# Gated MLP behind block attention on one core: a contiguous place for the low words' bits, and other places in the hand-written order for loads, scores and one weight part

## The chip, the cores and the metric

The kernel runs on one core of a Trainium2 chip. The metric is the device time of one execution in microseconds (us); the version before takes 528.58 us, the median of three runs (528.41 to 528.75). TensorE, VectorE, ScalarE, GpSimd and SyncE are called PE, DVE, ACT, POOL and SP, as in the profile; PEld is PE's loading of weights. SP issues all DMAs.

## What is computed

```python
# 8 batches, 8 heads, 576 tokens, head size 64: attention inside chunks of 64 tokens
scores = scale * np.matmul(q_c, k_c.transpose(0, 1, 2, 4, 3))
attn = np.exp(scores - np.max(scores, axis=-1, keepdims=True))
x = np.matmul(attn / (np.sum(attn, axis=-1, keepdims=True) + 1e-09), v_c)   # -> (8, 576, 512)
# then, for every batch
h = gelu_tanh(x @ w_in)                       # w_in (512, 1024), given in 64-bit floats
u, v = (h[..., :512], h[..., 512:])
v_n = (v - mean(v)) / np.sqrt(var(v) + 1e-06) * g_ln
v_s = np.einsum('ts,bsd->btd', w_sg, v_n) + b_sg[None, :, None]
out = x + (u * v_s) @ w_out                   # w_out (512, 512), given in 64-bit floats
```

## The kernel before

**Tiles and units.** Attention works on 36 tiles of 128 tokens, numbered 0 to 35; a batch has four and a half. The MLP works batch by batch, in units of 12 or 14 weight passes on PE: `v_unit` (L440, matmul L451), `u_unit` (L479, L488), `s_unit` (L500, L508) and `o_unit` (L520, L531). Each product of two 32-bit numbers is made of three passes with high and low parts, hence the names ending in `h` and `l`. A unit's result lies in one of three buffers named `pm` in PSUM, and the unit three places later waits until ACT or DVE has emptied it.

**The start.** Batches 0 and 1 are worked off by a list, START (L45). A letter and a number are a step: `v13` is `v_unit` of batch 1, part 3, and likewise `u`, `s`, `o`. `S` scores a tile (L313 or L321, then softmax), `T` transposes it, `O` multiplies by V (L409) and keeps the result (`keep`, L418: `xh`, `xl` and `xf`, on ACT and DVE). `P5` is `S` for tiles 5 and 6 together, `Q5` is `O` for both. `L`, `W`, `w` load, begin and end one of four parts of `w_in`'s v half, `X` and `x` begin and end one of its u half. `Y0` to `Y7` load and convert the eight parts of `w_out` (`o_w`, L213). `A8` loads tiles up to 8 where that has not been done. `D` is a run of spare matmuls (L577). From batch 2 on, loops run the units and a table, SLOTS, hangs attention steps behind them; neither is touched.

**Loads.** `att_load` (L281) takes one of four buffers `qkv_t`. `scores` (L550) loads two tiles ahead of the tiles that it scores, once the first batch is past. The parts of `w_out` go through the same four buffers (`st`, L219). A buffer is taken when its last reader is done, and SP issues in order: what waits for a buffer holds up every later DMA.

**Weights in 64-bit floats.** `pair_begin` (L152) makes of one part's words a 32-bit number `f`, its power of two `p`, and in L165 16-bit words `q` with the bits that `f` has lost. `pair_end` (L167) sums them on PE in four passes (L177): `f`, `q`, `p`, and minus the high part; ACT then writes `win_l` (L178). A u unit needs its own part's `win_l`.

**What orders the engines.** START gives the order in which steps are recorded. When the program is built, a scheduler places the instructions of each engine by readiness, so an engine's row differs from the list in places; on the chip, each engine then works its row off strictly in order.

Of the kernel before, what the change touches and what calls it, by code (L numbers as in the profile page):

```python
# [14 lines left out]
U16 = mybir.dt.uint16  # L15
BF16 = mybir.dt.bfloat16
AF = mybir.ActivationFunctionType
ALU = mybir.AluOpType
# [3 lines left out]
B, H, S, D = 8, 8, 576, 64  # L22
P = 128
# [20 lines left out]

START = """  # L45
L0 A0 A1 L1 S0 L2 T0 D11 A2 W0 A3 W1 L3 A4 S1 W2 S2 w0 w1 W3 T1 O0 w2 S3 O1 T2 w3 D14 O2 T3 S4 M0 v00 X0 O3 G0 T4 v01
A8 O4 x0 X1 v02 x1 X2 v03 v04 u00 g0 g1 x2 g2 u01 g3 X3 u02 x3 g4 u03 P5 s00 s01 T5 P7 s02 T6 Q5 s03 T7 T8 v10 Q7 v11
Y0 Y1 v12 Y2 v13 Y3 u10 Y4 u11 Y5 u12 Y6 u13 Y7 A10 s10 s11 P9 s12 s13 o00 T9 o01 T10 o02 o03 Q9 P11 o10 o11 T11 o12
T12 Q11 S13 o13 T13
"""  # L50

PE_TILES = 5
# [28 lines left out]
def block_attention_gated_mlp(ctx: ExitStack, tc: tile.TileContext, qkv, w_in, w_out, w_sg, g_ln, b_sg, out):  # L81
    nc = tc.nc
# [43 lines left out]
    def high_word(f, hw):  # L126

        nc.scalar.activation(f.bitcast(F32), hw.bitcast(F32), AF.Abs, scale=2.0**16)  # L130
        nc.vector.tensor_scalar(f.bitcast(F32), f.bitcast(F32), ZERO64, TOP64, op0=ALU.max, op1=ALU.min)
        nc.vector.tensor_scalar(f, f, 4, 1, op0=ALU.logical_shift_left, op1=ALU.logical_shift_right)
        nc.vector.scalar_tensor_tensor(f, hw, -0x80000000, f, op0=ALU.bitwise_and, op1=ALU.bitwise_or)
# [20 lines left out]
    def pair_begin(n, st):  # L154

        pair = st[:, : 2 * n].rearrange("p (n w) -> p n w", w=2)
        f, p = st[:, 2 * n : 3 * n], st[:, 3 * n : 4 * n]  # L160
        high_word(f, pair[:, :, 1])
        nc.vector.tensor_scalar(p, f, -0x800000, None, op0=ALU.bitwise_and)

        q, top = st[:, : 2 * n].bitcast(U16)[:, 1::4], p.bitcast(U16)[:, 1::2]
        nc.vector.scalar_tensor_tensor(q, q, 9, top, op0=ALU.logical_shift_right, op1=ALU.bitwise_or)  # L165

    def pair_end(n, hi, lo, st):  # L167

        f = st[:, 2 * n : 3 * n].bitcast(F32)
        p, q = st[:, 3 * n : 4 * n].bitcast(BF16)[:, 1::2], st[:, : 2 * n].bitcast(BF16)[:, 1::4]  # L170
        ps = ps_m.tile([P, 2, 512], F32, name="pm")[:, 0, :n]
        shape = lambda a: a.rearrange("p (k c) -> p k c", k=hi.shape[1]) if len(hi.shape) == 3 else a
        nc.scalar.mul(hi, shape(f), -1.0)
        terms = [(ident, f), (low[0], q), (low[1], p), (ident_r, hi)]
        for i, (a, c) in enumerate(terms):
            out_ps = shape(ps) if c is hi else ps
            nc.tensor.matmul(out_ps, a, c, start=(i == 0), stop=(i == len(terms) - 1))  # L177
        nc.scalar.mul(lo, shape(ps), -1.0)  # L178
# [14 lines left out]
    def v_w_end(kt):  # L193
        pair_end(DH, win_h[:, kt, DH:], win_l[:, kt, DH:], staged["v", kt])
        u_w_load(kt)
# [61 lines left out]
    def load_misc():  # L257
        nc.sync.dma_start(out=g_bc, in_=g_ln.broadcast_to([P, DH]))
# [4 lines left out]
    last = [((b + 1) * S - 1) // P for b in range(B)]  # L263
# [6 lines left out]
    def next_bank():  # L270
        turn[0] ^= 1
        return banks[:, turn[0]].rearrange("p (hp s) -> p hp s", hp=HP)
# [30 lines left out]
    def att_scores(*tiles):  # L303

        scs = []
        for i, t in enumerate(tiles):
            qt = state[t]
            if t < PE_TILES:
                sc = ps_m.tile([P, 2, H, D], F32, name="pm")[:, 0]
                for h in range(H):  # L310
                    for c in range(2):
                        r = slice(c * D, (c + 1) * D)
                        nc.tensor.matmul(sc[r, h, :], qt[r, 0, h, :], qt[r, 1, h, :], start=True, stop=True)  # L313
            else:


                sc = banks[:, :, i * HP * D : (i + 1) * HP * D].rearrange("p c (hp s) -> p c hp s", hp=HP)
                for h in range(H):
                    for c in range(2):
                        r, o = slice(c * D, (c + 1) * D), slice((h + c) % 2 * D, ((h + c) % 2 + 1) * D)  # L320
                        nc.tensor.matmul(sc[o, c, h // 2, :], qt[r, 0, h, :], qt[r, 1, h, :], start=True, stop=True)  # L321
            scs.append(sc)
        for t, sc in zip(tiles, scs):
            softmax_begin(t, sc)
        for t in tiles:
            softmax_end(t)

    def softmax_begin(t, sc):
        qt = state[t]
        nmax = small.tile([P, H], F32, name="nmax")  # L330
        by_slot = lambda a: a if t < PE_TILES else a.rearrange("p (c hp) s -> p c hp s", c=2)
        nc.vector.tensor_reduce(  # L332
            nmax if t < PE_TILES else nmax.rearrange("p (c hp) -> p c hp", c=2), sc, axis=AX.X, op=ALU.max, negate=True
        )
        pt = att.tile([P, H, D], F32, name="pt", bufs=3)
        den = small.tile([P, H], F32, name="den")
        scale = 1.0 / math.sqrt(D)
        if t in ACT_SOFTMAX:
            nc.vector.tensor_scalar(nmax, nmax, scale, None, op0=ALU.mult)
            for h in range(H):  # L340
                col = slice(h, h + 1)
                src = sc[:, h, :] if t < PE_TILES else sc[:, h // HP, h % HP, :]
                nc.scalar.activation(pt[:, h, :], src, AF.Exp, bias=nmax[:, col], scale=scale, accum_out=den[:, col])  # L343
        else:
            nc.vector.tensor_tensor(
                by_slot(pt), sc, by_slot(nmax.unsqueeze(2).broadcast_to([P, H, D])), op=ALU.add
            )
            nc.scalar.activation(pt, pt, AF.Exp, scale=scale)
        state[t] = (qt, pt, den)

    def softmax_end(t):
        qt, pt, den = state[t]
        if t not in ACT_SOFTMAX:
            nc.vector.tensor_reduce(den, pt, axis=AX.X, op=ALU.add)
        nc.vector.tensor_scalar(den, den, SM_EPS, None, op0=ALU.add)
        nc.vector.reciprocal(den, den)  # L356
        (nc.gpsimd if t > last[1] else pick(f"n{t}")).tensor_tensor(pt, pt, den.unsqueeze(2).broadcast_to([P, H, D]), op=ALU.mult)  # L357
        state[t] = (qt, pt)
# [25 lines left out]
    def att_out(*tiles):  # L384

        xos = []
        pm = ps_m.tile([P, 2, 512], F32, name="pm") if tiles[0] >= PE_TILES else None
        for i, t in enumerate(tiles):
            qt, ptT = state.pop(t)
            if t < PE_TILES:  # L390
                vt = qt[:, 2, :, :].rearrange("p (c hp) d -> p c hp d", c=2)
                xo = next_bank()
                for hp in range(HP):
                    for c in range(2):
                        for j in range(2):
                            r = slice(j * D, (j + 1) * D)
                            nc.tensor.matmul(
                                xo[r, hp, c * D : (c + 1) * D], vt[r, c, hp, :], ptT[r, hp, c * D : (c + 1) * D],
                                start=True, stop=True,
                            )  # L400
                xo = xo.rearrange("p hp (c s) -> p c hp s", c=2)
            else:

                xo = pm[:, :, i * HP * D : (i + 1) * HP * D].rearrange("p c (hp s) -> p c hp s", hp=HP)
                for h in range(H):
                    for c in range(2):
                        j, place = (h + c) % 2, c * HP + h // 2
                        r, o = slice(j * D, (j + 1) * D), slice(h % 2 * D, (h % 2 + 1) * D)
                        nc.tensor.matmul(  # L409
                            xo[o, c, h // 2, :], qt[r, 2, place, :], ptT[r, place].rearrange("p a s -> p (a s)"),  # L410
                            start=True, stop=True,
                        )
            xos.append(xo)
        for t, xo in zip(tiles, xos):
            keep(t, xo)
# [129 lines left out]
    def ahead(t):  # L545
        while loaded[0] <= min(t, NT - 1):
            att_load(loaded[0])
            loaded[0] += 1

    def scores(*tiles):  # L550
        if tiles[0] > last[0]:
            ahead(tiles[-1] + 2)
        att_scores(*tiles)

    def att_slots(b, n):
# [9 lines left out]

    steps = {
        "L": v_w_load, "M": lambda k: load_misc(), "W": v_w_begin, "w": v_w_end, "X": u_w_begin, "x": u_w_end, "A": ahead,
        "S": scores, "T": att_transpose, "O": att_out, "P": lambda t: scores(t, t + 1), "Q": lambda t: att_out(t, t + 1),
    }
    for name, f in zip("vuso", (v_unit, u_unit, s_unit, o_unit)):  # L570
        steps[name] = (lambda f: lambda k: f(k // 10, k % 10))(f)
# [65 lines left out]
```

## Time and profile before

The profiled execution took 529.45 us; its span, from the first to the last instruction, is 527.7 us, and every time of the trace counts from the span's start.

| | value |
|---|---|
| median of three runs | 528.58 us |
| profiled execution | 529.45 us |
| its span | 527.7 us |
| mean granted PE clock | 0.990 |
| ACT busy, share of the span | 275.3 us, 52% |
| POOL busy, share of the span | 71.9 us, 14% |
| DMA | 46.58 MB, mean 88 GB/s |

An engine's busy time is the sum of its instructions' spans. In a timeline each row gives a start, a length, the engine, the line and the operation; a bracket at its end gives how long the engine had been idle and what released it. Matmuls are pipelined: a unit's cost on PE is the distance between its first start and the next unit's first start.

### The profile page before, as it was taken

Reading aid. Unit: us, or ns where it says so; the run is one execution under the profiler, and the core shown is the slowest. Engines: PE = TensorE matmul, PEld = TensorE weight load, DVE = VectorE, ACT = ScalarE, POOL = GpSimd, SP = SyncE. Lnnn points to the kernel's source line nnn. Section 1 sums busy time; section 2 is a strip of 40 time slices with the busy share of each in tenths; the row PEclk is TensorE's granted clock in tenths of the full one; section 3 lists DMA queues with packets and bytes.
Section 4 is the critical chain, followed back from the end, with each engine's and each line's share of the span. In section 5 each row is a group of like instructions: output and inputs, shape, how many; then the busy total and the mean of one; then the engine's idle time right before and its main releaser. Section 6 shows DMA issues by size and latency. Waiting matters only on the chain.

```text
span 527.7 us, 12465 instructions
## 1 busy us (share of the span) xinstructions
PE 507.2 (96%) x5278; PEld 467.3 (89%) x5278; DVE 341.6 (65%) x704; ACT 275.3 (52%) x509; POOL 71.9 (14%) x75
## 2 busy tenths in 40 slices
PE   5989989799999989999999999999999999999997
PEld 5576869689999879998999889998999899998996
DVE  5978808877977676758655495768556495636042
ACT  4677634665434687535564367445654468324110
POOL 0032300011011131103110040103010040102000
PEclk9999989899999999999999999999999999999999
DMA  8676000412346700333214402251305300020002
GB/s 331 241 228 193 0 1 1 121 42 82 85 121 210 207 21 14 108 106 105 71 52 130 134 9 55 67 151 62 106 16 155 117 0 2 2 91 1 1 1 89
DMA packets 49595, 46.58 MB, mean 88 GB/s; under 512 B 35202, under 2 KB 39554, under 8 KB 49540
## 3 DMA queue, kind: packets, MB, share of 16 engines
q1 hardware_dynamic: 49540, 45.80, 28.8%
q8 instruction: 41, 0.67, 0.5%
q14 instruction: 14, 0.11, 0.1%
HBM read 36.34 MB, written 9.44 MB: 87 GB/s over the span
## 4 chain that ended last, share of the span: by engine, by line
PE 77%; DVE 10%; ACT 6%; issue 2%; POOL 2%; DMA 1%; DVEq 0%; SPq 0%; ACTq 0%; POOLq 0%
PE pm L508 21%; PE pm L488 19%; PE pm L531 17%; PE pm L451 14%; PE pm L409 3%; PE banks L321 2%; POOL sm L460 1%; ACT pt L343 1%; DMA qkv_t<-qkv 1%; DVE blocks L371 1%; DVE wsg L165 1%; DVE wout L165 1%; DVE nmax L332 1%; DVE sm L457 1%; ACT xh L94 1%
## 5 line engine op out<-in xcount | busy, mean ns | idle before, releaser
L508 PE MATMUL pm<-wsg,v 128*128 128x288 f32 x768 | 108.2, 296 | 0.0
L508 PEld LDWEIGHTS pm<-wsg,v 128*128 128x128 f32 x768 | 103.8, 189 | 0.5
L531 PE MATMUL pm<-gh,wout 128*128 128x288 f32 x512 | 92.1, 297 | 0.0
L531 PEld LDWEIGHTS pm<-gh,wout 128*128 128x128 f32 x512 | 76.0, 189 | 0.5
L357 POOL TENSOR_TENSOR pt<-pt,den 128x512 f32<-128x512 f32 x28 | 29.8, 1076 | 235.7 <-DVE den L356 125.8
L488 PE MATMUL pm<-xh,win_l 128*128 128x288 f32 x256 | 56.1, 301 | 3.8 <-ACT win_l L178 2.3
L460 POOL TENSOR_TENSOR sm<-sm,neg_half 128x1 f32<-128x1 f32 x36 | 35.3, 980 | 166.2 <-DVE sm L459 165.6
L531 PE MATMUL pm<-gl,wout 128*128 128x288 f32 x256 | 55.7, 296 | 0.0
L488 PE MATMUL pm<-xh,win_h 128*128 128x288 f32 x256 | 55.7, 299 | 0.0
L488 PE MATMUL pm<-xl,win_h 128*128 128x288 f32 x256 | 55.5, 298 | 0.0
L451 PE MATMUL pm<-win_h,xl 128*128 128x512 f32 x128 | 52.4, 409 | 2.1 <-DVE xl L97 2.1
L94 ACT CAST gh<-gt 128x576 fp32r<-128x576 f32 x32 | 21.5, 673 | 61.0 <-DVE gt L512 60.8
L451 PE MATMUL pm<-win_l,xh 128*128 128x512 f32 x128 | 51.5, 403 | 0.0
L451 PE MATMUL pm<-win_h,xh 128*128 128x512 f32 x128 | 51.5, 402 | 0.0
L512 DVE TENSOR_TENSOR gt<-pm,u 128x576 f32<-128x576 f32 x32 | 24.2, 756 | 37.9 <-PE pm L508 37.9
L488 PEld LDWEIGHTS pm<-xh,win_l 128*128 128x128 f32 x256 | 41.9, 191 | 5.2 <-ACT win_l L178 2.7
L539 DVE TENSOR_TENSOR ot<-pm,xf 128x576 f32<-128x576 f32 (+1 forms) x33 | 24.1, 734 | 28.9 <-PE pm L531 28.8
L488 PEld LDWEIGHTS pm<-xh,win_h 128*128 128x128 f32 x256 | 41.6, 191 | 0.0
L531 PEld LDWEIGHTS pm<-gl,wout 128*128 128x128 f32 x256 | 41.5, 189 | 0.1
L488 PEld LDWEIGHTS pm<-xl,win_h 128*128 128x128 f32 x256 | 41.6, 191 | 0.0
L457 DVE BATCH_NORM_STATS2 sm<-hs 128x6 f32<-128x512 f32 x36 | 24.7, 687 | 25.1 <-ACT hs L454 25.0
L97 DVE TENSOR_TENSOR xl<-pm,xh 128x512 fp32r<-128x512 f32 (+1 forms) x34 | 21.8, 641 | 26.3 <-ACT xh L94 26.3
(121 smaller groups left out, 843.1 us busy)
## 6 DMA issues: line engine op xcount, KB each, us to landing
qkv_t<-qkv SPq DMA_DIRECT2D x32, 512.0 KB, 4.5
out_dram<-ot SPq DMA_DIRECT2D x31, 288.0 KB, 2.2
qkv_t<-qkv SPq DMA_DIRECT2D x124, 64.0 KB, 3.7
qkv_t<-qkv SPq DMA_DIRECT2D x3, 768.0 KB, 9.7
wsg<-w_in SPq DMA_DIRECT2D x4, 512.0 KB, 4.1
wout<-w_in SPq DMA_DIRECT2D x4, 512.0 KB, 6.1
st<-w_out SPq DMA_DIRECT2D x8, 256.0 KB, 2.8
stage<-w_sg SPq DMA_DIRECT2D x5, 288.0 KB, 4.1
```

The source lines that it names most:

```text
L94: nc.scalar.copy(hi, src)
L97: lo_eng.tensor_tensor(lo, src, hi.bitcast(F32), op=ALU.subtract)
L357: (nc.gpsimd if t > last[1] else pick(f"n{t}")).tensor_tensor(pt, pt, den.unsqueeze(2).broadcast_to([P, H, D]), op=ALU.mult)
L409: nc.tensor.matmul(xo[o, c, h // 2, :], qt[r, 2, place, :], ptT[r, place].rearrange("p a s -> p (a s)"), start=True, stop=True,)
L451: nc.tensor.matmul(pv, a[:, kt, tok], c[:, kt, DH:], start=(i == 0), stop=(i == 11))
L457: nc.vector.bn_stats(st, h)
L460: nc.gpsimd.tensor_tensor(rs, rs, neg_half, op=ALU.pow)
L488: nc.tensor.matmul(pm[:, j, :HS], a[:, kt, dc], c[:, kt, j * HS : (j + 1) * HS], start=(i == 0), stop=(i == 11))
L508: nc.tensor.matmul(pm[:, j, :HS], a[:, dc], c[:, m, j * HS : (j + 1) * HS], start=(i == 0), stop=(i == len(ops) - 1))
L512: nc.vector.tensor_tensor(gt.rearrange("p (a c) -> p a c", a=2), pm[:, :, :HS], u2[0][:, dt, :].rearrange("p (a c) -> p a c", a=2), op=ALU ...
L531: nc.tensor.matmul(pm[:, j, :HS], a[:, kt, ec], c[:, kt, j * HS : (j + 1) * HS], start=(i == 0), stop=(i == len(ops) - 1),)
L539: nc.vector.tensor_tensor(ot[:, js], pm[:, js, :HS], res[:, js], op=ALU.add)
```

## The change

Three things are changed. L165 writes its 16-bit words into the first `n` half-words of the staging tile, side by side, where it wrote into the half-words that it read, eight bytes apart; `pair_end` reads them there. In START, `X3`, the beginning of `w_in`'s last u part, stands four steps earlier. `x2`, `x3`, the parts `g` of `w_sg`, `P5` to `P9` and `P11`, `Q7` and some `T` and `Y` steps have other places. And `S` and `P` in START load nothing any more: loads stand as steps of their own (`A10`, `A12`, `A14`, `A15`).

```diff
-Y0 Y1 v12 Y2 v13 Y3 u10 Y4 u11 Y5 u12 Y6 u13 Y7 A10 s10 s11 P9 s12 s13 o00 T9 o01 T10 o02 o03 Q9 P11 o10 o11 T11 o12
+Y0 v12 Y1 v13 Y2 u10 Y3 u11 Y4 u12 Y5 Y6 u13 Y7 A10 s10 A12 s11 P9 s12 s13 T9 o00 T10 P11 o01 o02 o03 Q9 A14 T11 o10
...
-        q, top = st[:, : 2 * n].bitcast(U16)[:, 1::4], p.bitcast(U16)[:, 1::2]
-        nc.vector.scalar_tensor_tensor(q, q, 9, top, op0=ALU.logical_shift_right, op1=ALU.bitwise_or)
+        words = st[:, : 2 * n].bitcast(U16)
+        q, lw, top = words[:, :n], words[:, 1::4], p.bitcast(U16)[:, 1::2]
+        nc.vector.scalar_tensor_tensor(q, lw, 9, top, op0=ALU.logical_shift_right, op1=ALU.bitwise_or)
...
-        p, q = st[:, 3 * n : 4 * n].bitcast(BF16)[:, 1::2], st[:, : 2 * n].bitcast(BF16)[:, 1::4]
+        p, q = st[:, 3 * n : 4 * n].bitcast(BF16)[:, 1::2], st[:, : 2 * n].bitcast(BF16)[:, :n]
...
     def scores(*tiles):
-        if tiles[0] > last[0]:
-            ahead(tiles[-1] + 2)
+        ahead(tiles[-1] + 2)
         att_scores(*tiles)
...
-        "S": scores, "T": att_transpose, "O": att_out, "P": lambda t: scores(t, t + 1), "Q": lambda t: att_out(t, t + 1),
+        "S": att_scores, "T": att_transpose, "O": att_out, "P": lambda t: att_scores(t, t + 1), "Q": lambda t: att_out(t, t + 1),
```

One line is added behind L163, so L165 is L166 in the changed kernel and every later line named here is one higher; helpers above it, and L577, keep their numbers. On DVE and ACT the rows are the same up to the softmax of tile 5, and on PE up to the end of `u01`. Three places follow.

PE before, from the last pass of `u02` to the first of `u03` (`wout_378` holds `w_in`'s fourth u part, `banks` the scores of tile 5):

```order
L488 MATMUL pm<-xh,win_h 128x288 x2
L177 MATMUL pm<-wout_378,ident 128x512
L177 LDWEIGHTS low_86
L177 MATMUL pm<-wout_378,low_86 128x512
L177 LDWEIGHTS low_87
L177 MATMUL pm<-wout_378,low_87 128x512
L177 MATMUL pm<-win_h,ident 128x512
L321 MATMUL banks<-qkv_t 64x64 x10
L488 MATMUL pm<-xh,win_l 128x288 x2
```

PE now, from the last pass of `u01` to the first of `u02`:

```order
L489 MATMUL pm<-xh,win_h 128x288 x2
L178 MATMUL pm<-wout_378,ident 128x512
L178 LDWEIGHTS low_86
L178 MATMUL pm<-wout_378,low_86 128x512
L178 LDWEIGHTS low_87
L178 MATMUL pm<-wout_378,low_87 128x512
L178 MATMUL pm<-win_h,ident 128x512
L489 MATMUL pm<-xh,win_l 128x288 x2
```

The fourth part's passes (step `x3`) have moved from behind `u02` to ahead of it, and all 32 rows of `P5` now stand between `u02` and `u03`.

PE before, from the end of `s03` to the first pass of `v10` (L321 scores tile 9, L409 is `Q5`'s tile 6):

```order
L508 MATMUL pm<-wsg_720,z_0_96 128x288 x2
L508 MATMUL pm<-wsg_719,z_0_94 128x288 x2
L321 MATMUL banks<-qkv_t 64x64 x4
L409 MATMUL pm<-ptT,qkv_t 64x64
L321 MATMUL banks<-qkv_t 64x64 x2
L409 MATMUL pm<-ptT,qkv_t 64x64 x15
L321 MATMUL banks<-qkv_t 64x64 x10
L451 MATMUL pm<-win_h,xl 128x512
```

PE now, at the same place:

```order
L509 MATMUL pm<-wsg_732,v 128x288 x2
L509 MATMUL pm<-wsg_733,z_0_96 128x288 x2
L509 MATMUL pm<-wsg_732,z_0_94 128x288 x2
L410 MATMUL pm<-ptT,qkv_t 64x64 x32
L452 MATMUL pm<-win_h,xl 128x512
```

The L410 rows are now `Q7` (tiles 7 and 8), which stood behind `v10`. `Q5` has moved up whole between `s01` and `s02`, and tile 9 is scored with tile 10 behind `s11`.

DVE now, ahead of those rows of PE, from the second `xl` of `Q5` to the copies that end the transposes of tiles 7 and 8; the rows with `st` begin the first part of `w_out`, which stood behind the statistics of `v10` and `v11` before:

```order
L97 TENSOR_TENSOR xl<-pm,xh 128x2x4x64
L131 TENSOR_SCALAR st<-st 128x256
L132 TENSOR_SCALAR st<-st 128x256
L513 TENSOR_TENSOR gt<-pm,u_723 128x576
L372 STREAM_TRANSPOSE blocks<-pt 128x512 x2
L97 TENSOR_TENSOR gl<-gt,gh 128x576
L382 COPY ptT<-blocks 32x8x32 x4
```

On SP, the eight loads of `w_out` have moved ahead of the loads of tiles 9 to 12: the order was tile 8, tiles 9 and 10, `w_out`, tiles 11 and 12, and is tile 8, `w_out`, tiles 9 to 12.

More of the change, by code (lines that the diff above doesn't have):

```diff
@@ L46 @@
 L0 A0 A1 L1 S0 L2 T0 D11 A2 W0 A3 W1 L3 A4 S1 W2 S2 w0 w1 W3 T1 O0 w2 S3 O1 T2 w3 D14 O2 T3 S4 M0 v00 X0 O3 G0 T4 v01
-A8 O4 x0 X1 v02 x1 X2 v03 v04 u00 g0 g1 x2 g2 u01 g3 X3 u02 x3 g4 u03 P5 s00 s01 T5 P7 s02 T6 Q5 s03 T7 T8 v10 Q7 v11
-Y0 Y1 v12 Y2 v13 Y3 u10 Y4 u11 Y5 u12 Y6 u13 Y7 A10 s10 s11 P9 s12 s13 o00 T9 o01 T10 o02 o03 Q9 P11 o10 o11 T11 o12
-T12 Q11 S13 o13 T13
+A8 O4 x0 X1 v02 x1 X2 v03 X3 v04 u00 x2 g0 g1 u01 x3 g2 g3 u02 P5 g4 u03 T5 s00 T6 P7 s01 Q5 s02 T7 T8 s03 Q7 v10 v11
+Y0 v12 Y1 v13 Y2 u10 Y3 u11 Y4 u12 Y5 Y6 u13 Y7 A10 s10 A12 s11 P9 s12 s13 T9 o00 T10 P11 o01 o02 o03 Q9 A14 T11 o10
+T12 o11 Q11 S13 A15 o12 T13 o13
 """
```

## The prediction

> **What bounds the kernel now.** I read first the page's busy shares (each digit a tenth of a fortieth of the span), then PE by stretches, then PE's waits, and only then the timelines.
>
> ```profile
> PE 507.2 (96%) x5278; PEld 467.3 (89%) x5278; DVE 341.6 (65%) x704; ACT 275.3 (52%) x509; POOL 71.9 (14%) x75
> ...
> PE   5989989799999989999999999999999999999997
> ...
> PEclk9999989899999999999999999999999999999999
> ```
>
> PE is busy for 507.2 of 527.7 us, so at most 20.5 us can come from idle time. Both rows dip only in the first slices. In the rows by stretches, the length comes first, then busy time and count of PE, PEld, DVE, ACT and POOL, then the granted clock.
>
> ```profile
> 68.30:73.20 4.90, 4.90 (x25) 4.90 (x26) 0.00 (x0) 0.48 (x1) 0.00 (x0) 0.66 0.00 0
> 80.11:103.50 23.39, 20.32 (x275) 19.05 (x276) 21.83 (x45) 12.27 (x22) 0.00 (x0) 0.94 0.23 63
> 97.30:108.60 11.30, 8.26 (x141) 6.27 (x141) 6.81 (x15) 8.86 (x16) 0.00 (x0) 0.70 0.32 82
> 111.00:196.00 85.00, 82.75 (x852) 76.34 (x851) 67.17 (x157) 49.24 (x92) 12.18 (x13) 1.00 0.39 113
> 211.00:528.00 317.00, 312.87 (x3204) 297.89 (x3203) 186.44 (x368) 149.33 (x247) 42.22 (x42) 1.00 0.23 68
> ```
>
> From 211 us on PE is busy for 312.87 of 317.00 us at a clock of 1.00, and the change touches nothing there. The losses that can be won back lie before: idle PE, and stretches at a clock of 0.66 and 0.70, where busy time itself is too long. PE's waits with their releaser (total, times, longest) name the places:
>
> ```profile
> PE pm L488 <- ACT win_l L178: 2.3, 2, 2.1
> PE pm L451 <- DVE xl L97: 2.1, 1, 2.1
> PE pm L488 <- ACT hs L454: 1.5, 1, 1.5
> PE pm L409 <- ACT ptT L379: 1.0, 3, 0.5
> ```
>
> **Step A, 0 to 36 us: L165.** Two groups by line (busy time, mean ns), then pieces of the chain that ended last:
>
> ```profile
> L165 DVE SCALAR_TENSOR_TENSOR wsg<-wsg 128x512 uint16<-128x512 uint16 x4 | 5.2, 1304 | 0.0
> L133 DVE SCALAR_TENSOR_TENSOR wsg<-wsg 128x512 int32<-128x512 int32 x4 | 2.7, 686 | 0.0
> ...
> 8.51 1.21 DVE wsg L165
> ...
> 17.21 1.22 DVE wsg L165
> ...
> 20.96 1.21 DVE wout L165
> ...
> 35.46 1.23 DVE wsg L165
> ```
>
> L133 is the same instruction over as many elements. It reads words eight bytes apart, as L165 does, but writes them side by side, and takes 0.69 us for 1.30. By elimination the spread output is what costs, and the change removes just that: 0.62 us less for each of eight. Four lie on the chain. The first saves little: PE scores tile 1 only behind 22 spare matmuls, which stay. Of the other three, 1.86 us, I take −1.0, because in the same stretch ACT and POOL have chains of their own close behind (both ends: −1.9, if all of it counts, and +0.2, if 16-bit words pack worse than 32-bit ones). In L177 the pass that reads `q` streams the same 512 columns; I cost it at nothing.
>
> [...]
>
> **Step B, to the first `s00` pass.** PE's timeline (start, length, operation, count, idle time before), and one row of ACT:
>
> ```profile
> 61.06 1.02 PE L177 MATMUL pm<-wout,ident 128*128 128x512 f32 x2
> ...
> 62.83 0.42 PE L488 MATMUL pm<-xh,win_l 128*128 128x288 f32 x2
> ...
> 65.75 0.43 PE L488 MATMUL pm<-xh,win_h 128*128 128x288 f32 x2
> ...
> 68.30 0.54 PE L488 MATMUL pm<-xh,win_l 128*128 128x288 f32 x2 [2.12 <-ACT win_l L178]
> ...
> 73.03 1.12 PE L177 MATMUL pm<-wout,ident 128*128 128x512 f32 x2
> ...
> 79.99 3.45 PE L508 MATMUL pm<-wsg,v 128*128 128x288 f32 x24
> ```
> ```profile
> 67.67 0.58 ACT L178 ACTIVATE win_l<-pm 128x512 fp32r<-128x512 f32 x1
> ```
>
> `u02` waits until 68.30 for a `win_l` that ACT writes at 67.67 to 68.25, behind other work that the change leaves in place. So its start stays. But the 1.77 us of `x3`'s passes (61.06 to 62.83 is `x2`'s, of one size) now fill the gap from 66.02 on, and about 0.5 us of idling is left. Then `u02` runs as `u01` does, in 3.2 to 3.3 us instead of 4.73: the lowered clock (0.66) came behind the idle 2.12, and 0.5 is a quarter of that. Behind it come `P5`'s 64 passes whole, 1.1, and `u03`, 3.3, for which `x3`'s `win_l` is long there. `s00`: 68.30 + 3.3 + 1.09 + 3.3 = 75.99 instead of 79.99, **−4.0**.
>
> **Step C, from `s00` to `v11`.**
>
> ```profile
> 87.63 1.16 PE L321 MATMUL banks<-qkv_t 64*64 64x64 f32 x64
> ...
> 97.97 0.34 PE L321 MATMUL banks<-qkv_t 64*64 64x64 f32 x8 [0.70 <-DMA qkv_t<-qkv]
> 98.62 0.27 PE L409 MATMUL pm<-ptT,qkv_t 64*64 64x64 f32 x1 [0.31 <-ACT ptT L379]
> ...
> 102.15 0.80 PE L451 MATMUL pm<-win_h,xl 128*128 128x512 f32 x1 [2.06 <-DVE xl L97]
> ...
> 107.50 1.16 PE L409 MATMUL pm<-ptT,qkv_t 64*64 64x64 f32 x64
> 108.60 0.50 PE L451 MATMUL pm<-win_h,xl 128*128 128x512 f32 x1
> ...
> 111.50 0.40 PE L451 MATMUL pm<-win_h,xl 128*128 128x512 f32 x1
> ```
> ```profile
> 80.11 0.69 DVE L332 TENSOR_REDUCE nmax<-banks 128x8 f32<-128x512 f32 x1 [12.81 <-PE banks L321]
> ...
> 102.90 0.60 DVE L381 COPY ptT<-blocks 32x256 f32<-32x256 f32 x2 [0.17 <-ACT ptT L374]
> ```
>
> Before, this takes 28.61 us: four `s` units, tiles 7 and 8 scored, `Q5`, tile 9, a wait of 2.06 for `Q5`'s `xl`, `v10` at half speed (5.35 instead of 2.9: the clock of 0.70 follows this sparse stretch), and `Q7`. Now PE has the four `s` units 15.5 (two stand from 79.99 to 87.63, 7.64; doubled, with 0.1 for each step to other work), `P7` 1.1, `Q5` 1.1, `Q7` 1.1, `v10` 2.9 (as from 108.60 to 111.50): 21.7. The scores of tile 9, their wait for a DMA and the wait for `xl` are gone from here, since `Q5` is two units earlier. What is late next is **`Q7`**, which needs the transposes of tiles 7 and 8. DVE took from 80.11 to 103.50, 23.4 us (21.83 busy), for the softmax of tiles 5 to 8, the products `gt` and `gl` and the transposes' copies. The same list now starts when `P5` is done, 72.7, and would end at 96.1; queued up from its rows, with the two leading rows of `w_out` (0.6 on DVE, 1.6 on ACT) ahead of `gt`, it ends at 95.8 on ACT, whose swaps are last. PE is at `Q7`'s first half at 93.7 and starts it at about 95: a wait of some 1.8 in all. Behind it on PE stand `v10` to `v13`, so all of it counts. Sum: 21.7 + 1.8 = 23.5, **−5.1** (ends: −6.9 without the wait; −0.6 with 2.0 more and `v10` still slow).
>
> [...]
>
> **Step D, `v12`.** It began at 111.50 without a wait. Its PSUM buffer is now that of `Q7`, whose last `xf` stands on ACT behind a table load and `hs`. Queued from their rows, it ends 1.0 us late: **+1.0** (0 to +1.5).
>
> **Step E, 117 to 195 us.** The loads of `w_out` (least, median and longest issue in ns, first and last start), the page's row of a tile's first load (count, KB, us to landing), and rows of SP, ACT and PE in order of time:
>
> ```profile
> L222 SPq DMA_DIRECT2D st<-w_out x8: 367/368/416, 108.3 to 136.4; - x8
> ```
> ```profile
> qkv_t<-qkv SPq DMA_DIRECT2D x32, 512.0 KB, 4.5
> ```
> ```profile
> 142.02 0.34 SPq L296 DMA_DIRECT2D qkv_t<-qkv  x1
> ...
> 146.62 0.35 SPq L296 DMA_DIRECT2D qkv_t<-qkv  x1
> ...
> 188.47 1.28 ACT L454 ACT_TABLE_LOAD   x1
> ...
> 195.28 0.54 PE L488 MATMUL pm<-xh,win_l 128*128 128x288 f32 x2 [1.53 <-ACT hs L454]
> ```
>
> `u20` waits 1.53 because ACT changes tables between exp and `hs` around it; with tiles 11 and 12 scored between `o00` and `o01`, that exp is done long before. Two waits on `ptT` there (0.15 and 0.52) go too. Tile 9's scores move here, +0.55, and `Q11` waits about 0.65 for tile 12's copies. Sum −2.2 + 1.2 = **−1.0** (−2.2 to +1.0).
>
> Loads: the first part of `w_out` can issue when `Q5` has freed a buffer, about 85.4; at the old pace the eighth issues 28.1 us later, at 113.5. Before, the two loads behind it were issued 5.6 and 10.2 us after it (136.4), so tile 10's comes at 123.7 and lands, at the page's 4.5 us, by 128.2. PE reaches `P9` at about 129.5: hidden, by 1.3 us.
>
> **Sum.** −1.0 − 4.0 − 5.1 + 1.0 − 1.0 = −10.1. The execution of 529.45 would be 519.3; it stands 0.87 above the median of 528.58, so the predicted median is **518.5**.
>
> **Rivals.**
> - R1, the words are no faster: the hopping read of 16-bit words costs, not the write, and L166 stays at 1.30. For it: 16-bit operands on both sides, which L133 has not. 519.5. [...]
> - R2, `Q7` becomes the new slow place. DVE is busy 21.83 of 23.39 us in the stretch, with hardly any slack, so any slip goes straight to `Q7`. Two us more make its gap 3.8, more than the 2.12 that was followed by the slow clock; `v10` then costs 2.5 more, and `v12`'s 1.0 goes: 518.5 + 2.0 + 2.5 − 1.0 = 522.0.
> - R3, slower than before: tiles 9 and 10 are loaded behind the whole of `w_out`, whose parts wait for buffers that DVE and ACT free. Each us that tile 10 lands behind 129.5 is a us on PE, which has nothing to put in its place. From 139.6 on the gain of 10.1 is eaten. If the parts are held to PE's progress, so that the eighth issues only 9 us earlier than before, 127.4, tile 10 lands at 127.4 + 10.2 + 4.5 = 142.1: 12.6 us of waiting, 531.
> - R4, no change: the waits for `win_l`, `xl` and `hs` only change places, since ACT and DVE were the cause, and both slow stretches stay: 528.5. Against it: DVE idles 12.81 us ahead of 80.11, which an earlier `P5` fills.
> - R5, better: the waits at `Q7` and `v12` don't come, 518.5 − 2.8 = 515.7.
>
> **Numbers.** The forecast 50% (its own range 516.5 to 520.5), R1 17%, R2 17%, R3 6%, R4 5%, R5 5%. The range goes from R5 with 0.7 more of step A, 515.0, to R2 with R1 and a us of waiting at `P9`, 524.0; R3, R4 and a little of the tails stay out. A measurement of this kernel can tell about 0.2%, 1.06 us, from no change. Faster are the forecast, R1, R2 and R5, 0.89; same R4, 0.05; slower R3, 0.06.
>
> **What would show it.** A: L166 at about 690 ns, not 1304. B: `u02` with a wait of 0.5 or less, a clock near 1.00 there, `s00` at about 75. C: no wait for `xl` or a DMA ahead of `v10`, one of 1.8 at `Q7` for `ptT`, `v10` in 2.9. D: `v12` waiting about 1.0 for `xf`. E: `P9` not waiting for a DMA, `u20` not waiting. It is wrong if PE shows a slow clock behind `Q7`, or DMA waits at `P9`.

## The result and the profile after

| | before | changed |
|---|---|---|
| median (lowest to highest, 4 runs each) | 528.5 us (527.5 to 528.75) | 515.77 us (514.95 to 516.12) |
| ratio, 95% interval | | 0.976 (0.9742 to 0.9779) |
| profiled execution, its span | 529.45, 527.7 us | 516.12, 514.3 us |

The changed kernel is 2.4% faster. The forecast was 518.5 us; the time lies 2.7 us below it, inside the stated range (515.0 to 524.0) and below the forecast's own (516.5 to 520.5). The page of the changed kernel: the first two rows of busy time, PE in fortieths of the span, and the granted clock.

```profile
PE 500.4 (97%) x5273; PEld 464.8 (90%) x5278; DVE 337.0 (66%) x704; ACT 274.4 (53%) x509; POOL 73.7 (14%) x75
...
PE   5989999899999999999999999999999999999997
...
PEclk9999999899999999999999999999999999999999
```

PE is idle for 13.9 us instead of 20.5, and busy for 6.8 us less. Part of that is less work at a low clock: ahead of the kernel's end the clock stood at 0.50 for 3.41 and 6.83 us before (from 69.82 and from 100.54), and for 3.41 now (from 93.76). Part is also the shorter passes of L178 (below) and rows of attention that stand together again. PE's waits, with what ended them:

```profile
PE pm L314 <- DMA qkv_t<-qkv: 5.7, 1, 5.7
PE pm L410 <- ACT ptT L380: 1.5, 1, 1.5
PE banks L366 <- ACT xf L428: 1.5, 2, 0.8
PE pm L489 <- ACT win_l L179: 0.7, 1, 0.7
PE pm L178 <- DVE wout L133: 0.4, 1, 0.4
```

The waits for `xl`, for `hs` and for a DMA at the scores of tile 9 are gone, the one for `win_l` has shrunk from 2.1 to 0.7, and one of 1.5 us for `ptT` has come: that is `Q7`. Where the time went is best read from the first pass of each stage on PE:

```profile
34.66 0.50 PE L452 MATMUL pm<-win_h,xl 128*128 128x512 f32 x1
54.70 0.43 PE L489 MATMUL pm<-xh,win_l 128*128 128x288 f32 x2
...
62.62 1.02 PE L178 MATMUL pm<-wout,ident 128*128 128x512 f32 x2
...
65.06 0.53 PE L489 MATMUL pm<-xh,win_l 128*128 128x288 f32 x2 [0.74 <-ACT win_l L179]
...
72.83 3.35 PE L509 MATMUL pm<-wsg,v 128*128 128x288 f32 x24
...
91.94 1.94 PE L410 MATMUL pm<-ptT,qkv_t 64*64 64x64 f32 x64 [1.47 <-ACT ptT L380]
93.81 0.80 PE L452 MATMUL pm<-win_h,xl 128*128 128x512 f32 x1
...
98.23 0.40 PE L452 MATMUL pm<-win_h,xl 128*128 128x512 f32 x1
...
106.63 0.43 PE L489 MATMUL pm<-xh,win_l 128*128 128x288 f32 x2
...
181.94 0.43 PE L489 MATMUL pm<-xh,win_l 128*128 128x288 f32 x2
```

These rows are the starts of `v00`, `u00`, `x3`, `u02`, `s00`, `Q7`, `v10`, `v11`, `u10` and `u20`. Beside the same starts before:

| stretch | before, us | changed, us | difference | forecast |
|---|---|---|---|---|
| A, start to `u00` | 57.86 | 54.70 | -3.16 | -1.0 |
| B, `u00` to `s00` | 22.13 | 18.13 | -4.00 | -4.0 |
| C, `s00` to `v11` | 28.61 | 25.40 | -3.21 | -5.1 |
| D, `v11` to `u10` | 8.50 | 8.40 | -0.10 | +1.0 |
| E, `u10` to `u20` | 78.18 | 75.31 | -2.87 | -1.0 |
| `u20` to the end | 332.42 | 332.36 | -0.06 | 0 |
| span | 527.70 | 514.30 | -13.40 | -10.1 |

So the sum is off by 3.3 us, and it hides larger errors of both signs: A, D and E too small a gain, C too large. The stretches by windows (length, busy of PE, PEld, DVE, ACT, POOL, then the clock) show C's loss:

```profile
65.06:72.83 7.77, 7.77 (x112) 7.54 (x113) 3.09 (x5) 3.91 (x6) 0.00 (x0) 1.00 0.01 2
91.94:98.20 6.26, 6.06 (x76) 4.88 (x77) 6.10 (x18) 4.58 (x11) 0.00 (x0) 0.73 0.31 91
98.23:106.60 8.37, 8.37 (x37) 6.76 (x36) 7.72 (x22) 7.13 (x15) 1.85 (x2) 1.00 0.31 92
```

The slow clock behind `win_l`'s wait has gone (1.00 where it was 0.66), but one stands behind `Q7`'s wait: `v10` takes 4.42 us, 93.81 to 98.23, instead of 2.9. `Q7` itself takes 1.87 us instead of 1.1, because its second tile's copies come late too. Two groups on DVE and one on PE (busy, mean ns) complete the picture, of the changed kernel:

```profile
L133 DVE SCALAR_TENSOR_TENSOR wsg<-wsg 128x512 int32<-128x512 int32 x4 | 2.7, 686 | 0.0
L166 DVE SCALAR_TENSOR_TENSOR wsg<-wsg 128x512 uint16<-128x512 uint16 x4 | 2.7, 682 | 0.0
...
L178 PE MATMUL pm<-wsg,low 128*128 128x512 bf16 x6 | 2.0, 383 | 0.0
```

L166 takes 682 ns where L165 took 1304. The third row was not in the forecast; before, it was

```profile
L177 PE MATMUL pm<-wsg,low 128*128 128x512 bf16 x8 | 3.4, 510 | 0.3 <-DVE den L355 0.3
```

Two of the eight records are missing from the later row. The surer figure is the distance from a part's first pass to the next unit: 57.89 to 59.43 in the changed kernel, 1.54 us instead of 1.77.

### The profile page after: what moved, and what is told of

It is laid out like the page before. It is cut to its first block, busy times and chain, and to the rows that moved or that the text cites. A ratio compares the mean times of both kernels' runs of the same rounds, so it can differ in the third digit from the quotient of the medians.

```text
span 514.3 us, 12454 instructions
## 1 busy us (share of the span) xinstructions
PE 500.4 (97%) x5273; PEld 464.8 (90%) x5278; DVE 337.0 (66%) x704; ACT 274.4 (53%) x509; POOL 73.7 (14%) x75
## 4 chain that ended last, share of the span: by engine, by line
PE 83%; DVE 6%; ACT 5%; POOL 2%; issue 2%; DMA 1%; DVEq 0%; SPq 0%; POOLq 0%; ACTq 0%
PE pm L509 21%; PE pm L532 19%; PE pm L489 19%; PE pm L452 17%; PE pm L410 3%; PE banks L322 3%; POOL sm L461 1%; PE pm L577 1%; DMA qkv_t<-qkv 1%; DVE nmax L333 1%; PE pm L314 1%; ACT ptT L380 1%; ACT ptT L375 1%; POOL xl L97 1%; ACT pt L344 0%
```

## The experiments

The theory behind them: the words and the order are two separate gains; the order's gain is that each wait of PE is filled with work that is ready; and what is left is `Q7`, where ACT and DVE are behind.

### Words and order apart

The order alone (the old line in the changed kernel):

```diff
-        words = st[:, : 2 * n].bitcast(U16)
-        q, lw, top = words[:, :n], words[:, 1::4], p.bitcast(U16)[:, 1::2]
+        q, top = st[:, : 2 * n].bitcast(U16)[:, 1::4], p.bitcast(U16)[:, 1::2]
...
```

> The changed order with the old line: the low words' bits are written over the half-words that were read, eight bytes apart, and read so. Theory (the words are worth 3.2 us before u00, of which step A had only 1.0; the order is worth the rest): DVE's instruction is back at 1.30 us, the four passes of a part back at 1.77 us on PE instead of 1.54, u00 starts at about 57.9 instead of 54.7, and the time is 515.8 + 3.2 = 519.0 us. Rival (the gain ahead of u00 comes from the order of DVE and ACT, not from the words): u00 starts at about 54.7 and the time is 515.8 to 516.3.

Measured 518.31 us (518.26 to 519.34; ratio 0.9828, 0.9809 to 0.9846). `u00` starts at 57.69, a part's passes take 1.77 us (60.89 to 62.66), by PE's timeline:

```profile
57.69 0.43 PE L488 MATMUL pm<-xh,win_l 128*128 128x288 f32 x2
...
60.89 1.02 PE L177 MATMUL pm<-wout,ident 128*128 128x512 f32 x2
...
62.66 0.42 PE L488 MATMUL pm<-xh,win_l 128*128 128x288 f32 x2
```

The words alone (the new line in the kernel before, whose START and loads stay as they were):

```diff
-        q, top = st[:, : 2 * n].bitcast(U16)[:, 1::4], p.bitcast(U16)[:, 1::2]
+        words = st[:, : 2 * n].bitcast(U16)
+        q, lw, top = words[:, :n], words[:, 1::4], p.bitcast(U16)[:, 1::2]
...
```

> The old order with the new line alone. Theory (words and order add up): u00 starts at about 54.7, everything after it is 3.2 us earlier with the same waits, 528.5 - 3.2 = 525.3 us. Rival (the old order gives the gain back in its waits for win_l, xl and hs, because ACT or a DMA sets their ends): 527.5 us or more.

Measured 524.28 us (523.18 to 524.82; ratio 0.9935, 0.9911 to 0.996). `u00` starts at 54.97, and the large old waits are there, 3 to 5 us earlier: 2.26 us for `win_l`, 2.06 for `xl`, 1.51 for `hs`. The ratios multiply to 0.9764, against 0.976 measured for both together. Within the intervals the two parts add up, and neither is taken back by the other.

The distance between the words, four bytes instead of eight or two:

```diff
-        q, lw, top = words[:, :n], words[:, 1::4], p.bitcast(U16)[:, 1::2]
+        q, lw, top = words[:, : 2 * n : 2], words[:, 1::4], p.bitcast(U16)[:, 1::2]
...
```

> The changed kernel, but the bits are written and read four bytes apart (in every second half-word) instead of side by side. Theory (any place that is not side by side costs on both engines): DVE at about 1.3 us, the four passes on PE at 1.77, 519.0 us. Rival 1 (only the distance of eight bytes costs): 0.68 us, 1.54 us and 515.8. Rival 2 (a cost that grows with the distance): DVE near 0.95 us, some 517.4.

Measured 515.3 us (514.79 to 516.02), no different from the changed kernel. Rival 1 held: DVE's instruction, in the groups by line, takes

```profile
L166 DVE SCALAR_TENSOR_TENSOR wsg<-wsg 128x512 uint16<-128x512 uint16 x4 | 3.0, 742 | 0.0
```

and the passes of a part 1.55 us (57.50 to 59.05). So "side by side" was too strong. A step of four bytes costs 0.06 us on DVE and 0.01 on PE; it is the step of eight that cost 0.62 and 0.23. On DVE the old line also wrote over the very half-words that it read, and no run separates that from the step. L133 writes over one of its operands too, side by side, and takes 0.69 us, so writing in place is not enough to make it slow.

### The gap ahead of `u02`

```diff
-... u00 x2 g0 g1 u01 x3 g2 g3 u02 P5 g4 u03 ...
+... u00 x2 g0 g1 u01 g2 g3 u02 x3 P5 g4 u03 ...
```

> The changed kernel with step x3 put back behind u02, all else as changed. Theory (x3's passes fill a gap whose end ACT sets): u02 starts where it does now, at about 65.0, after 2.3 us of idling instead of 0.74, a slow clock follows it (u02 in 4.7 us instead of 3.4), and x3's 1.54 us are paid behind it: 515.8 + 1.3 + 1.5 = 518.6 us. Rival (the gap isn't filled but moved, since the wait at Q7 takes up what is lost here or ACT's row gets shorter ahead of win_l): 515.8 to 516.5.

Measured 518.87 us (517.29 to 519.04; ratio 0.9827, 0.9805 to 0.9848). The wait is back at 2.27 us and `x3` is paid behind `u02`: from `u00` to `s00` it takes 19.67 us instead of 18.13, just `x3`'s 1.54 more, so the gap is really filled by the new place. (`X3`, which has `x3`'s words ready in time, stands eight steps earlier in START than before, not four.) PE's timeline, then the window of `u02`:

```profile
64.70 0.53 PE L489 MATMUL pm<-xh,win_l 128*128 128x288 f32 x2 [2.27 <-ACT win_l L179]
...
67.99 1.02 PE L178 MATMUL pm<-wout,ident 128*128 128x512 f32 x2
```

By windows:

```profile
64.70:67.99 3.29, 3.29 (x25) 3.29 (x26) 0.00 (x0) 0.48 (x1) 0.00 (x0) 1.00 0.00 0
```

But in this profiled execution, the fastest of the four runs (517.29), `u02` runs at a clock of 1.00 behind the gap. The other three runs, 518.87 to 519.04, have a mean clock of 0.992 or 0.993 where this one has 0.996. That fits one slow stretch more in those three, for the one of this profile lies at `Q7`; of those only the mean clock is known. The last section comes back to it.

### `Q7`: the gap and the clock

`Q7` back behind `v10`:

```diff
-... s03 Q7 v10 v11 ...
+... s03 v10 Q7 v11 ...
```

> The changed kernel with Q7 behind v10 again, all else as changed. Theory (PE reaches Q7 before ACT has its copies; v10 needs nothing that is late): v10 starts right behind s03, at about 90.4 instead of 93.8, runs in 2.9 us, Q7 follows without a wait, v11 starts at about 94.4 instead of 98.2; 515.8 - 3.8 = 512.0 us, or 513.7 where the runs of the changed kernel had no slow clock behind Q7. Rival (the wait moves: v12 or v13 then wait for Q7's xl and xf, behind v10's statistics on ACT and DVE): 515 to 516.

Measured 516.78 us (516.62 to 517.47): no gain, and a little over the rival's 516. The rival's wait came true, for `xl` at `v12`: `v10` and `Q7` run without a wait, and `v12` then waits longer than `Q7` had, with a slow clock behind it. PE's timeline:

```profile
90.21 0.40 PE L452 MATMUL pm<-win_h,xl 128*128 128x512 f32 x1
...
93.10 1.16 PE L410 MATMUL pm<-ptT,qkv_t 64*64 64x64 f32 x64
94.19 0.50 PE L452 MATMUL pm<-win_h,xl 128*128 128x512 f32 x1
...
99.88 0.50 PE L452 MATMUL pm<-win_h,xl 128*128 128x512 f32 x1 [2.62 <-DVE xl L97]
```

By windows:

```profile
99.88:104.30 4.42, 4.42 (x12) 3.49 (x13) 4.02 (x11) 3.42 (x8) 0.79 (x1) 0.61 0.26 83
```

PE kept busy in the gap instead:

```diff
...
+        for _ in range(8 if tiles[0] == 7 else 0):
+            nc.tensor.matmul(pm[:, 0, :P], ident, ident, start=True, stop=True)
...
```

> The changed kernel with eight spare matmuls at the head of Q7, into Q7's own buffer, so that PE is busy while it waits; the result is overwritten by Q7. Theory (v10 and Q7 are slow in the profile of the changed kernel because PE idled for 1.47 us before them): Q7 starts where it does, takes 1.1 instead of 1.87 us, v10 2.9 instead of 4.4, 515.8 - 2.3 = 513.5 us. Rival (the slow stretch comes at a time of the chip's own and not of the gap): 515.0 to 516.0, with a slow stretch of the same cost somewhere or nowhere.

Measured 518.14 us (516.67 to 518.23), above both expectations. The stretch from the spare matmuls through `v11` has a clock of 1.00, as the theory wanted; but so it has in the changed kernel's second profile (below), where nothing fills the gap, so this doesn't show that the spare matmuls did it. `Q7` still takes 1.62 us, 91.82 to 93.44, and 1.87 in that second profile at a clock of 1.00: its length is the late second tile and not the clock. And `v12` waits 2.12 us for `hs`, with the slow clock there. PE's timeline at `v12`, ACT's row that it waited for, and the windows ahead of `v12` and behind:

```profile
101.43 0.50 PE L454 MATMUL pm<-win_h,xl 128*128 128x512 f32 x1 [2.12 <-ACT hs L457]
...
100.78 0.60 ACT L457 ACTIVATE hs<-pm 128x512 f32<-128x512 f32 x1
```

By windows:

```profile
89.94:99.10 9.16, 9.06 (x106) 7.50 (x104) 8.12 (x22) 6.03 (x14) 0.00 (x0) 1.00 0.27 86
101.43:107.00 5.57, 5.57 (x17) 4.47 (x18) 4.81 (x13) 4.61 (x11) 1.84 (x2) 0.69 0.15 49
```

More than PE's row moved here. On ACT one cast of `w_out` more stands ahead of each `xh` of `Q7` (the first `xh` begins at 95.67, at 94.02 in the second profile of the changed kernel), and the `hs` above begins at 100.78 instead of 99.04. What a filled gap alone is worth, this run can't say.

What moving `Q7` shows: ACT and DVE set `v12`'s start. It came at 99.88, against 99.69 in the changed kernel's second profile, though PE was done with `v11` some 2 us earlier. What PE gains ahead of `v12` is lost there again; what it loses ahead of `v12` is free only as far as that wait reaches.

### The tail of batch 1

The steps from `o00` on as before, all else changed:

```diff
-... T9 o00 T10 P11 o01 o02 o03 Q9 A14 T11 o10 T12 o11 Q11 S13 A15 o12 T13 o13
+... o00 T9 o01 T10 o02 o03 Q9 P11 o10 A14 o11 T11 o12 T12 Q11 S13 A15 o13 T13
```

> The changed kernel with the steps from o00 on as before: T9 and T10 one unit later, P11 behind Q9, T11 and T12 later. Theory (u20 waited because exp and hs of the same stretch each change ACT's table; P11's earlier place took that away, and the waits for ptT with it): the waits of 0.15, 0.52 and 1.53 us come back at about the same lengths, 515.8 + 2.2 = 518.0 us, or + 2.9 = 518.7 if the torn units of o cost what they did. Rival (the waits went because everything ahead of them was earlier, or because of w_out's place in SP's row): 515.5 to 516.3.

Measured 518.44 us (518.05 to 519.56; ratio 0.9821, 0.9798 to 0.9844). Two of the waits are back at their old length (the one of 0.15 isn't listed), and from `o00` (135.63) to `u20` it takes 49.65 us instead of 46.32. PE's timeline:

```profile
163.16 0.32 PE L410 MATMUL pm<-ptT,qkv_t 64*64 64x64 f32 x2 [0.52 <-ACT ptT L380]
...
185.28 0.54 PE L489 MATMUL pm<-xh,win_l 128*128 128x288 f32 x2 [1.52 <-ACT hs L455]
```

The 1.52 and the 0.52 us account for 2.0 of the 3.3. The rest, by subtraction, is eight rows of tile 16 that stand ahead of `u20` again (0.34) and attention rows that stand one by one between rows of `o` and `v`. So many steps moved at once that the run doesn't show which of them ended the wait for `hs`.

### What stands ahead of `v12`: the loads' place

If ACT and DVE are the bound there, `w_out`'s conversion is what can move: in the changed kernel it ended at 122.6 us, and `o00` starts at 135.6. Tiles 9 and 10 loaded ahead of it take two of the four buffers, so that it starts later:

```diff
-... P7 s01 Q5 s02 ... Y7 A10 s10 ...
+... P7 s01 Q5 A10 s02 ... Y7 s10 ...
```

> The changed kernel with tiles 9 and 10 loaded ahead of w_out again (A10 behind Q5), all else as changed: w_out then has two buffers fewer and begins some 12 us later. Theory (w_out's rows, moved ahead on SP, stand in the queues of ACT and DVE ahead of Q7's copies and of v10 to v12's work): Q7's wait falls from 1.47 to about 0.7 us, since 1.7 us of ACT and 0.6 of DVE go from ahead of it; 515.0 us. Rival 1 (these rows lie in gaps of ACT and DVE): the wait stays at 1.5, 515.8. Rival 2 (with two buffers w_out ends behind 135 us and o00 waits for it): over 516.5.

Measured 519.1 us (518.54 to 519.8). As expected `Q7`'s wait fell (0.93 us), and `u10` starts at 104.61 instead of 106.63 (105.39 in the changed kernel's second profile, which has no slow clock at `v10` either). But `P11` then waited 2.7 us for tile 12, loaded behind the later `w_out`: a place that none of the expectations had named. With `Q7` behind `v10` as well:

```diff
-... s03 Q7 v10 v11 ...
+... s03 v10 Q7 v11 ...
```

> As the kernel with tiles 9 and 10 loaded ahead of w_out, and Q7 behind v10 besides. Theory (what gave back the gain of Q7 behind v10 was v12's wait of 2.62 us for xl, because w_out's rows and v10's statistics stood ahead of it, and a slow clock of 1.5 us behind that wait): no wait at Q7, v12 waits under 1 us, no slow clock, u10 starts at about 104 instead of 106.6; 513.2 us. Rival (ACT and DVE have as much to do with or without w_out's rows, table load and hs ahead of xl being the larger part): v12 waits 2 us or more and the time is 515 to 517.

Measured 518.07 us (516.66 to 518.37). The stretch did better than the theory: no wait at all from `s00` on, `u10` at 102.49, 2.9 us earlier than in the changed kernel's second profile. What lost it again is `P11` and a slow clock behind its wait. PE's timeline, and the window of the `o` units that follow:

```profile
102.49 0.43 PE L489 MATMUL pm<-xh,win_l 128*128 128x288 f32 x2
...
138.32 0.90 PE L322 MATMUL banks<-qkv_t 64*64 64x64 f32 x32 [2.85 <-DMA qkv_t<-qkv]
```

By windows:

```profile
139.15:150.22 11.07, 11.07 (x76) 10.91 (x72) 8.26 (x17) 3.11 (x7) 2.09 (x2) 0.87 0.21 81
```

And `P9` in the gap, from the kernel with the earlier loads:

```diff
-... s03 Q7 v10 v11 ... s11 P9 s12 ...
+... s03 P9 Q7 v10 v11 ... s11 s12 ...
```

> As the kernel with tiles 9 and 10 loaded ahead of w_out, and P9 (the scores of both) put into the gap ahead of Q7 besides. Theory (the gap costs its own length, PE has nothing else to do there): the 1.09 us of P9 leave the stretch of s10 to s13 and Q7's wait falls to under 0.5 us, 514.0 us or less. Rival (the softmax of tiles 9 and 10 then stands on ACT and DVE ahead of xl, gl and the statistics, which set v12's start): a wait of 2 us or more for xl or hs at v12 or v13, 516 us or more.

Measured 521.13 us (520.64 to 522.27). The rival held: no wait at `Q7`, and `v12` waits 2.46 us for `hs`; `P11` waits 3.78 for its load besides.

### A version that beats both

The kernel with early loads and `Q7` behind `v10`, and `P11` at a place that its load can meet:

```diff
-... T9 o00 T10 P11 o01 o02 o03 Q9 ...
+... T9 o00 T10 o01 o02 P11 o03 Q9 ...
```

> The kernel with tiles 9 and 10 loaded ahead of w_out and Q7 behind v10, and P11 put behind o02 instead of o00. Theory (its only new loss was P11, which waited 2.85 us for tile 12, loaded behind w_out, and had a slow clock of 1.3 us behind it): u10 at 102.5 as there, no DMA wait, u20 without a wait, and 2.85 + 0.2 + 1.3 us less than there: about 512.5 us. Rival (the wait moves on, to T11's copies at Q11 or to hs at u20, since P11's exp is nearer to v20 now): 514.5 to 516.

Beside it ran the changed kernel with nothing edited:

> The changed kernel itself, beside the kernel that may beat it, on the same chip. Every theory: 515 to 516 us.

Measured 513.45 us (513.27 to 514.0; ratio 0.9724, 0.9707 to 0.9742) beside 514.87 us (514.7 to 515.95; ratio 0.9751, 0.9732 to 0.977) for the changed kernel on the same chip. The slowest run of the one is faster than the fastest of the other, by 0.7 us; the intervals of the two ratios overlap, because the kernel before scatters more than either. The DMA wait and `hs` at `u20` are gone, and two small waits are new among PE's:

```profile
PE pm L410 <- ACT ptT L380: 0.6, 1, 0.6
PE pm L532 <- DVE gt L513: 0.6, 1, 0.6
```

The first is `Q11`, which the later `P11` brings close to its copies. Together these 1.2 us are about what keeps it 1 us above the 512.5 expected.

The changed kernel's second profile is of use by itself. In it `Q7` waits as long as in the first, and no slow clock follows; `v12` then waits for `hs`. PE's timeline there, and two rows of ACT:

```profile
91.59 1.94 PE L410 MATMUL pm<-ptT,qkv_t 64*64 64x64 f32 x64 [1.46 <-ACT ptT L380]
...
99.69 0.50 PE L452 MATMUL pm<-win_h,xl 128*128 128x512 f32 x1 [0.35 <-ACT hs L455]
...
99.04 0.60 ACT L455 ACTIVATE hs<-pm 128x512 f32<-128x512 f32 x1
99.54 0.58 ACT L432 COPY xf<-pm 128x512 f32<-128x512 f32 x1
```

By windows:

```profile
91.59:97.82 6.23, 6.03 (x83) 4.87 (x84) 6.07 (x18) 4.55 (x11) 0.00 (x0) 1.00 0.30 87
```

Its span is 513.1 us, 1.2 less than that of the first profile. From `s00` to `v11` it takes 23.89 us instead of 25.40, so the slow `v10` cost 1.5; from `v11` to `u10` it takes 9.01 instead of 8.40, so 0.6 came back at `v12`. The other 0.35 had been gained by `u00` (54.35 against 54.70), where nothing differs but the execution.

## Why the prediction held, and where it failed

The direction, the place (nothing behind `u20`) and the main mechanism of each step were right. That the stated range held is in part luck: the forecast's own range missed the time, and the low end came from R5, whose condition (no wait at `Q7` and `v12`) did not come true. A, D and E brought 5.1 us more than forecast, C 1.9 less. Step by step:

- **A, forecast -1.0, measured -3.16.** The duration was right: 0.69 forecast for L166, 0.68 measured; the spread output was the cause, and R1 falls. Two terms failed. "I take −1.0, because in the same stretch ACT and POOL have chains of their own close behind" halved the sum for nothing: by `v00` 1.56 of the 1.86 had arrived (1.30 with the words alone, `v00` at 34.92). And the step stopped at 36 us, while the earlier DVE also ended a wait of 0.94 us for `xh` at 44.06: the order alone keeps that wait (0.96), the words alone don't.
- **"In L177 the pass that reads `q` streams the same 512 columns; I cost it at nothing"** was wrong. The passes of a part take 0.23 us less, and `x0` and `x1` stand between the units of `v` on PE in full: 0.47 us of A's 3.16 (1.56 by `v00`, 1.13 with the wait for `xh`, 0.47 here).
- **B, forecast -4.0, measured -4.00.** `u02` waited 0.74 for 0.5 and ran at full clock; putting `x3` back brought the 2.27 us. The shorter passes of `x2` and `x3` gave nothing here: ACT's `win_l` sets `u02`'s start (10.36 us behind `u00`'s, 10.44 before), so they only lengthen the wait.
- **C, forecast -5.1, measured -3.21.** The wait at `Q7` was right in place and near in size: 1.47 us of idling and 0.78 inside `Q7`'s rows, 2.25 for 1.8 in all. What failed is `v10` at 2.9: half of R2 came true in this profile, 4.42 us. In the second profile, where `v10` takes 2.92, C is -4.72. The row of a slow stretch behind 2.12 us was the right one to distrust that gap: here one of 1.47 us was followed by a slow stretch (0.50 from 93.76 to 97.17) that made `v10` 1.5 us longer. R2's condition, a gap of 3.8, was not needed, and the slow stretch did not come in every execution.
- **D, forecast +1.0, measured -0.10**, or +0.51 in the second profile, without the slow `v10`. The engine was right (ACT, behind a table load of 1.28 us, at 98.10 in the first profile); in the first profile the slow `v10` simply covered the wait. What ended it was not `Q7`'s last `xf`, as forecast: that ran until 100.12, and `v12` had begun at 99.69, right behind `v10`'s `hs`. C and D are not two terms but one: whichever of them loses, the other loses less. Moving `Q7` and the two profiles of the changed kernel show it.
- **E, forecast -1.0, measured -2.87.** The waits of 2.2 us went, and putting the tail back returned 2.0 of them. Tile 9's scores (0.55) and `Q11`'s wait came as forecast, the latter inside its rows: they take 1.57 us, some 0.5 more than `Q9`'s. The side gains were left out: 0.34 us of tile 16's scores that now stand behind `u20` and, by subtraction, some 1.4 us from rows of attention no longer torn into single rows among those of `o` and `v`.
- **Loads, R3 and R4.** No wait of `P9` for a DMA: tile 10's load was issued at 122.3 us (123.7 forecast), and `P9` began at 126.97, when by the 4.5 us of the profile's page it had just landed (126.8, an estimate from a median). There was little slack, and the kernels with `w_out` later show what happens without it, at `P11`: 2.7 to 3.8 us. R4 falls; only at `Q7` and `v12` does a wait change places.

## What to carry to other kernels

When a unit waits, ask what is ready that has to be done anyway, and put it there: `x3` in the gap gained its own length (1.54 us); spare matmuls in a gap were not seen to gain anything. Before counting a removed wait as a gain, find the next thing that the same slow engines must deliver; here a wait at `Q7` and one at `v12` were one and the same debt of ACT and DVE, and it only shrank when their work was moved elsewhere. Cost an access pattern with a wide step on every engine that touches the data: the eight bytes here were paid by DVE, which wrote (1.30 us an instruction against 0.68), and by PE, which read (1.77 us a part against 1.54).

## What the runs showed of the hardware that was not expected

- **PE paid for the step of what it streamed.** A 16-bit operand with a step of eight bytes made a part's passes 0.23 us longer than one with four or two bytes (1.77, 1.55, 1.54 us). On DVE the same write took 1.30, 0.74 and 0.68 us.
- **The same short gap was followed by a slow clock in one execution and not in another.** Gaps of 1.46 and 1.47 us at the same place of the same kernel: a clock of 1.00 behind the one, 0.73 behind the other. Gaps of 2.26 and 2.27 us at `u02` were followed by 1.00, one of 2.12 there by 0.66. A slow stretch cost a run 1.0 to 1.6 us (the spread between the runs of one kernel). It also explains the scatter: runs of the changed kernel with a mean clock of 1.000 took 514.70 to 514.95 us, those with 0.996 took 515.95 to 516.12.

The traces show a pattern in it. In all 14 profiles the clock's records begin whole multiples of 3.413 us apart, and each slow stretch ahead of the kernel's end lasts 3.413 us, two of them twice that, at a clock of 0.50. Where this grid lies against the span's start differs from execution to execution. By windows cut along it, at `Q7`, two of the first profile and three of the second:

```profile
90.34:93.76 3.42, 1.75 (x66) 1.35 (x64) 3.26 (x9) 2.68 (x6) 0.00 (x0) 1.00 0.00 0
93.76:97.17 3.41, 3.41 (x16) 2.71 (x9) 3.41 (x10) 2.41 (x6) 0.00 (x0) 0.50 0.51 154
...
87.54:90.95 3.41, 2.59 (x20) 2.36 (x18) 3.38 (x7) 3.00 (x7) 0.00 (x0) 1.00 0.00 0
90.95:94.37 3.42, 2.58 (x68) 2.12 (x69) 3.26 (x12) 2.68 (x7) 0.00 (x0) 1.00 0.14 37
94.37:97.78 3.41, 3.41 (x17) 2.73 (x16) 3.34 (x9) 2.42 (x7) 0.00 (x0) 1.00 0.40 121
```

In the first, PE idles for 1.67 us of one window, and the next is slow; in the second the same gap is split over two windows, 0.82 and 0.84, and none is slow. So it is at `u02`: 1.90 us in one window before, slow; 1.61 and 0.65 with the words alone, not slow. Over all profiles, ahead of the kernel's end, PE idled for 1.65 us or more of 11 windows at full clock, and a slow one followed each time; it followed one of the others, 1.46 us in the kernel before (97.13 to 100.54). This was read from the profiles afterwards, and no run set the place of the grid, so the bound is open.
